# Gated attention with a channel mix: attention in 64-token halves, the fourth head pair packed into padding rows, the first group left unsplit, and all engines in one planned order

## The chip, the cores and the metric

The kernel runs on one core of a Trainium2 chip. The metric is the device time of one execution in microseconds (us), the median of several runs. The engines are TensorE (PE, matmuls), VectorE (DVE), ScalarE (ACT) and GpSimd (POOL), and each works through its own instructions in order; SyncE (SP) issues most DMAs, also in order.

## The reference

Eight heads of 48 features, four batches of 768 tokens. Per head a 48x48 state decays by `alpha` along its rows and takes up `k v^T`; the output is `q` times the state. The eight heads' outputs, side by side, are the 384 features of a channel mix.

```python
for t in range(S):                                     # attention, per batch and head
    state = alpha[t][:, None] * state + outer(k[t], v[t])
    y[t] = q[t] @ state
xk = mu_k * x + (1 - mu_k) * x_prev                    # x: y of all heads, x_prev: one token before
xr = mu_r * x + (1 - mu_r) * x_prev
k = maximum(xk @ w_k, 0)                               # 384 -> 1024
v = (k * k) @ w_v                                      # 1024 -> 384
out = sigmoid(xr @ w_r) * v
```

## The kernel before

**Groups and chunks.** The 768 tokens of a batch are six chunks of 128 tokens. Chunks form groups (`CUTS`): 2, 2, 2 in the first batch, then 3, 3 in each of the others, nine groups in all. Heads go in pairs: one head on partitions 0 to 47, the other on 64 to 111, so a tile has 112 rows (`R`), and there are four pairs (`NP`).

**Preparation of a group** (`prep_p`, `prep_gh`). A scan over the tokens gives the running product of alpha (L231), a reverse scan its inverse (L254); q and k are multiplied by these (L249, L257). Tables in `PARAM` say which products run on DVE and which on POOL. After it a chunk needs matmuls and a causal mask only.

**Attention of a chunk** (`attn`). `scores` (L318): for each pair and head a matmul of 48 rows, 128 stationary and 128 moving columns, so that the two heads use the upper and the lower rows of the array. DVE multiplies all 1024 columns by the mask (L329). `trans` (L339): four transposes of k, copied by ACT (L342). `intra` (L391; L384 in the first group): eight matmuls over 128 tokens, whose outputs are 48 or 64 columns of the array for one head and for the other. `update` (L349): eight matmuls of 48 columns, added to the state by DVE (L357). `inter` (L407): four matmuls of 112 rows with a block-diagonal state. ACT copies the result to `xt` (L417) and the fourth pair to `x3` (L416), from where two DMAs put it into the 16 free rows behind each head (L420); the first group has a form of its own without these DMAs. All attention matmuls are f32.

**Channel mix of a group** (`mix`, `moe`). ACT scales (L474), DVE adds the previous token (L479), and each x is split into a rounded part (ACT, L482) and a remainder (L484). Weights are split likewise (`split`): merge (L186), rounding (L192, L194), remainder (L195, on POOL or DVE). Each product is then three matmuls on the fast f32r form: `up` (L501), `gate` (L526), `down` (L541). Between `up` and `down`, ACT and DVE square and split again (L509 to L515). The result is gated (L546) and stored (L547).

**Order.** PE's and SP's instructions are written out by hand. At the start 22 small matmuls on zeros are issued (L98). Attention of group g+1 is woven into the channel mix of group g by weights (`merge`); in the first group, weight splits and preparations are put in at fixed positions (`PARAM['pos']`), and 19 pieces of the second group's attention and then 14 of the first group's channel mix are issued ahead of the weaving. The other engines' order is that of the calls.

Of the kernel before, what the change touches and what calls it, by code (L numbers as in the profile page):

```python
# [25 lines left out]
C = 128  # L26
CUTS = [[2, 2, 2], [3, 3], [3, 3], [3, 3]]
GROUPS = [(b, sum(cut[:i]), n) for b, cut in enumerate(CUTS) for i, n in enumerate(cut)]
NG = len(GROUPS)
GMAX = 3 * C  # L30
# [3 lines left out]
NT = 3  # L34
NF = FF // 128
# [5 lines left out]
LEAD = 12.0  # L41
PARAM = {'pos': {'wk0': 29, 'wk1': 65, 'wk2': 22, 'wk3': 29, 'wr0': 106, 'wr1': 94, 'wv0': 70, 'wv1': 75, 'wv2': 72, 'wv3': 81, 'prep10': 12, 'prep11': 61, 'prep12': 65, 'prep13': 1, 'prep20': 104, 'prep21': 92, 'prep22': 102, 'prep23': 138, 'load2': 93, 'pp1': 88, 'pp2': 118}, 'dma': ['k', 'wk0', 'al', 'wk1', 'q', 'wk2', 'wk3', 'v'], 'eng': {'wr1': 'DP', 'wk0': 'AP', 'wk2': 'AP', 'wv0': 'DP', 'wv1': 'DP', 'wv2': 'AD', 'wv3': 'DP', 'wv4': 'DD', 'wv5': 'DD', 'wv6': 'DD', 'wv7': 'DD', 'wk1': 'AD', 'wk3': 'AP', 'wk4': 'DP', 'wk5': 'DP', 'wk6': 'DP', 'wk7': 'DP', 'wr0': 'DP', 'wr2': 'AD', 'wr3': 'AD', 'wr4': 'AD', 'wr5': 'AD', 'wr6': 'AD', 'wr7': 'AD'}, 'a1': 19, 'hold': 14, 'lead0': 8.0, 'sp': 3.0, 'prep': 0.2, 'xl': 'DDD', 'k2': 'AAD', 'h': ['DDDD', 'PDPD', 'PPPP'], 'm': 'AAA', 'warm': 22, 'g': ['PDDD', 'DPDP', 'DDDP'], 'sc': 'PP', 'mm': 2, 'direct': 1, 'pad': [1.0, 1.5], 'xr': 'DDD'}
NX = HB - D


def merge(main, side, lead):
    total = max(sum(w for w, _ in main) - lead, 1.0)
    load = sum(w for w, _ in side)
    done = spent = 0.0
    side = list(side)  # L50
    for w, f in main:
        f()
        done += w
        while side and spent / load <= done / total:
            ws, fs = side.pop(0)
            fs()
            spent += ws
    for _, fs in side:
        fs()
# [3 lines left out]
def gated_attention_channel_mix(  # L63
# [3 lines left out]
    q_p: bass.AP,  # L67
    k_p: bass.AP,
# [11 lines left out]
    nc = tc.nc  # L80
    PE, ACT, DVE, POOL = nc.tensor, nc.scalar, nc.vector, nc.gpsimd

    cp = ctx.enter_context(tc.tile_pool(name="cp", bufs=1))
    p1 = ctx.enter_context(tc.tile_pool(name="p1", bufs=1))
    p2 = ctx.enter_context(tc.tile_pool(name="p2", bufs=2))
    p3 = ctx.enter_context(tc.tile_pool(name="p3", bufs=3))
    ps = ctx.enter_context(tc.tile_pool(name="ps", bufs=1, space=PSUM))
    pm = ctx.enter_context(tc.tile_pool(name="pm", bufs=3, space=PSUM))
    dp = ctx.enter_context(tc.tile_pool(name="dp", bufs=1, space=DRAM))

    sbd = [cp.tile([R, NP, R], F32, name=f"sbd{i}") for i in range(2)]
    for t in sbd:
        POOL.memset(t, 0.0)

    hot = pm.tile([R, R], F32, tag="pm", name="hot")
    with tc.manual_schedule(engines={mybir.EngineType.PE}):
        for i in range(PARAM["warm"]):
            PE.matmul(hot, sbd[1][:, 0], sbd[1][:, 0], start=True, stop=True)  # L98

    tiny = cp.tile([128, 1], F32, name="tiny")  # L100
    POOL.memset(tiny, FLOOR)
    mone = cp.tile([128, 1], F32, name="mone")
    POOL.memset(mone, -1.0)
    ones = cp.tile([128, 1], F32, name="ones")
    POOL.memset(ones, 1.0)
    ACT.activation(ones, ones, AF.Sigmoid)
    POOL.memset(ones, 1.0)
    racc = cp.tile([128, 2 * NG], F32, name="racc")
    pbeg = cp.tile([128, NG * NP], F32, name="pbeg")
    pend = cp.tile([128, NG * NP], F32, name="pend")  # L110
    pscl = cp.tile([128, NG * NP], F32, name="pscl")
    mu = cp.tile([128, 2, NT], F32, name="mu")

    loaded = {}

    def span(g):
        b, c0, n = GROUPS[g]
        return b, c0, n, n * C

    def load(g):  # L120
        b, c0, nck, n = span(g)
        al = p2.tile([R, NP, n + 1], F32, tag="al", name=f"al{g}")
        pp = p1.tile([R, NP, n], F32, tag="pp", name=f"pp{g}")
        k = p2.tile([R, NP, n], F32, tag="k", name=f"k{g}")
        q = p2.tile([R, NP, n], F32, tag="q", name=f"q{g}")
        v = p2.tile([C, nck, NP, R], F32, tag="v", name=f"v{g}")
        loaded[g] = (al, pp, k, q, v)
        at = NP * (b * S + c0 * C)
        c1 = (b * S) // C + c0

        def get(t, src, p, m):
            nc.sync.dma_start(
                t[:, p : p + m, :n],
                src[:, at + p * n : at + (p + m) * n].rearrange("r (p t) -> r p t", p=m),
            )

        parts = {
            "al": lambda p=0, m=NP: get(al, al_p, p, m),
            "k": lambda p=0, m=NP: get(k, k_p, p, m),
            "q": lambda p=0, m=NP: get(q, q_p, p, m),  # L140
            "v": lambda: nc.sync.dma_start(v, v_p[:, c1 : c1 + nck]),
        }
        if g == 0:
            for p in range(0, NP, 2):
                for x in ("al", "k", "q"):
                    parts[x](p, 2)
            parts["v"]()
        elif g > 1:
            for x in parts:
                parts[x]()  # L150
        return parts

    with tc.manual_schedule(engines={mybir.EngineType.SP}):
        load(0)

    mask = cp.tile([C, C], F32, name="mask")
    POOL.memset(mask, 1.0)
    POOL.affine_select(
        out=mask, in_=mask, pattern=[[1, C]], compare_op=ALU.is_ge, fill=0.0,
        base=0, channel_multiplier=-1,  # L160
    )
    ident = cp.tile([128, 128], F32, name="ident")
    make_identity(nc, ident)
    wkh = cp.tile([128, NT, FF], F32R, name="wkh")
    wkl = cp.tile([128, NT, FF], F32R, name="wkl")
    wvh = cp.tile([128, NF, DM], F32R, name="wvh")
    wvl = cp.tile([128, NF, DM], F32R, name="wvl")
    wrh = cp.tile([128, NT, DM], F32R, name="wrh")
    wrl = cp.tile([128, NT, DM], F32R, name="wrl")

    tops = [cp.tile([128, 2 * DM], U32, name=f"tops{i}") for i in range(2)]
    for t in tops:
        POOL.memset(t, 0)
    turn = [0]

    def split(hi, lo, raw, he, le):
        w = raw.bitcast(U32)[:, :, 1::2]
        n = w.shape[2]
# [638 lines left out]
```

## Time and profile before

| | |
|---|---|
| runs | 403.24, 403.93, 401.58 us |
| median | 403.24 us |
| profiled execution, first to last instruction (span) | 396.4 us; its whole time is not given apart |
| PE busy | 356.6 us (90%) |
| DVE busy | 287.6 us (73%) |
| ACT busy | 190.0 us (48%) |
| POOL busy | 72.4 us (18%) |
| mean granted clock of PE | 0.947 |

A busy share is the time in which at least one instruction of the engine was under way. Matmuls are pipelined, so their durations overlap and the spacing of their starts says what one costs. An f32 matmul is recorded twice. "[idle before <-X]" says how long the engine stood still ahead of an instruction and what released it.

### The profile page before, as it was taken

To read this page: it belongs to the slowest core of one execution; us is meant where nothing else is said; L and a number is where in the kernel's file an instruction comes from. 1 tells how busy PE (TensorE), PEld (TensorE's weight loads), DVE (VectorE), ACT (ScalarE), POOL (GpSimd) and SP (SyncE) were. 2 spreads that over 40 slices of the span, in tenths; PEclk is the share of its full clock that TensorE was granted. 3 is DMA by queue.
4 is the path that set the end of the run, shared out by engine and by line. 5 is a ranking of instruction groups with operands and counts; after the bars stand their busy time and mean duration, and the time that the engine had idled before them with its cause. 6 is when DMAs were issued, how large, how long until landed. Compare 5 with 4: busy or idle time off the path is not lost.

```text
span 396.4 us, 7183 instructions
## 1 busy us (share of the span) xinstructions
PE 356.6 (90%) x2834; PEld 337.8 (85%) x2834; DVE 287.6 (73%) x451; ACT 190.0 (48%) x421; POOL 72.4 (18%) x85
## 2 busy tenths in 40 slices
PE   7674987898929979999999999999999999999993
PEld 7563976787919969999989999899999999999993
DVE  5699999996995399965998399929894755374510
ACT  3256874645613474444555446436644524463500
POOL 4364465361120030400040004000210000000000
PEclk9685998789988999999999999999999999999997
DMA  8997078537030611333112510251000100001001
GB/s 211 247 339 299 1 215 224 147 103 219 20 90 2 195 32 40 80 115 102 61 34 82 182 40 21 71 154 41 21 2 17 40 21 2 15 24 38 2 21 46
DMA packets 15816, 35.82 MB, mean 90 GB/s; under 512 B 1568, under 2 KB 9440, under 8 KB 15776
## 3 DMA queue, kind: packets, MB, share of 16 engines
q1 hardware_dynamic: 14608, 34.21, 28.8%
q10 hardware_dynamic: 1168, 1.09, 1.1%
q8 instruction: 24, 0.39, 0.4%
q14 instruction: 16, 0.13, 0.1%
HBM read 29.49 MB, written 4.72 MB: 86 GB/s over the span
## 4 chain that ended last, share of the span: by engine, by line
PE 46%; DVE 35%; DMA 9%; issue 4%; ACT 3%; SPq 1%; ACTq 0%; DVEq 0%
PE pv L541 14%; PE pk L501 14%; DVE al L254 6%; PE pg L526 5%; DVE pp L231 5%; DVE x L479 4%; DMA xt<-x 4%; DVE kl L515 4%; PE py L407 4%; PE py L391 4%; DMA al<-al_p 3%; PE sp L318 3%; DVE am L329 3%; DVE q L249 2%; DVE xkl L484 2%
## 5 line engine op out<-in xcount | busy, mean ns | idle before, releaser
L541 PE MATMUL pv<-wvl,kh 128*128 128x384 f32 x192 | 65.9, 343 | 2.9 <-DVE wvl L195 2.9
L541 PE MATMUL pv<-wvh,kl 128*128 128x384 f32 x192 | 65.6, 342 | 1.9 <-DVE kl L515 1.9
L541 PE MATMUL pv<-wvh,kh 128*128 128x384 f32 x192 | 65.9, 343 | 1.1 <-ACT r L509 1.1
L509 ACT ACTIVATE r<-pk 128x384 f32<-128x384 f32 (+1 forms) x72 | 32.6, 457 | 62.3 <-PE pk L501 45.4
L515 DVE TENSOR_TENSOR kl<-k,kh 128x384 fp32r<-128x384 f32 (+1 forms) x72 | 45.4, 630 | 7.6 <-ACT kh L514 2.8
L318 PE MATMUL sp<-q,k 48*128 48x128 f32 x384 | 33.2, 312 | 18.7 <-DVE am L329 14.0
L501 PE MATMUL pk<-xkh,wkh 128*128 128x384 f32 (+1 forms) x216 | 46.8, 325 | 1.9 <-ACT xkh L482 1.4
L318 PEld LDWEIGHTS sp<-q,k 48*128 48x128 f32 x384 | 26.8, 207 | 25.4 <-DVE am L329 15.9
L501 PE MATMUL pk<-xkh,wkl 128*128 128x384 f32 (+1 forms) x216 | 47.9, 331 | 0.0
L501 PE MATMUL pk<-xkl,wkh 128*128 128x384 f32 (+1 forms) x216 | 47.5, 329 | 0.0
L257 POOL TENSOR_TENSOR k<-k,al 112x768 f32<-112x768 f32 (+1 forms) x18 | 31.7, 1762 | 74.3 <-DVE al L254 47.3
L254 DVE TENSOR_TENSOR_SCAN al<-al 112x383 f32<-112x383 f32 (+1 forms) x36 | 41.1, 1176 | 1.0 <-ACT junk L238 0.7
L513 DVE TENSOR_TENSOR k<-r 128x384 f32<-128x384 f32 (+1 forms) x56 | 30.0, 536 | 16.1 <-ACT r L509 14.0
L479 DVE SCALAR_TENSOR_TENSOR x<-xt,nu,x 128x384 f32<-128x384 f32 (+1 forms) x54 | 31.2, 605 | 11.2 <-ACT x L474 11.1
L541 PEld LDWEIGHTS pv<-wvl,kh 128*128 128x128 f32 x192 | 36.6, 191 | 3.2 <-DVE wvl L195 3.2
L541 PEld LDWEIGHTS pv<-wvh,kl 128*128 128x128 f32 x192 | 36.5, 190 | 2.5 <-DVE kl L515 2.5
L501 PEld LDWEIGHTS pk<-xkh,wkh 128*128 128x128 f32 x216 | 36.4, 192 | 2.4 <-ACT xkh L482 1.6
L541 PEld LDWEIGHTS pv<-wvh,kh 128*128 128x128 f32 x192 | 36.6, 190 | 1.6 <-ACT r L509 1.4
L474 ACT ACTIVATE x<-xt,mu 128x384 f32<-128x384 f32 (+1 forms) x54 | 29.3, 577 | 17.5 <-DMA xt<-x 10.2
L501 PEld LDWEIGHTS pk<-xkh,wkl 128*128 128x128 f32 x216 | 36.1, 194 | 1.0
L501 PEld LDWEIGHTS pk<-xkl,wkh 128*128 128x128 f32 x216 | 35.8, 192 | 0.7 <-issue 0.4
L249 DVE TENSOR_TENSOR q<-q,pp 112x768 f32<-112x768 f32 (+1 forms) x20 | 15.9, 808 | 27.5 <-DMA q<-q_p 27.5
(93 smaller groups left out, 574.5 us busy)
## 6 DMA issues: line engine op xcount, KB each, us to landing
out<-sig SPq DMA_DIRECT2D x24, 192.0 KB, 1.8
k<-k_p SPq DMA_DIRECT2D x6, 672.0 KB, 4.4
al<-al_p SPq DMA_DIRECT2D x6, 672.0 KB, 5.1
q<-q_p SPq DMA_DIRECT2D x6, 672.0 KB, 6.4
v<-v_p SPq DMA_DIRECT2D x6, 672.0 KB, 5.0
wkraw<-wk_p SPq DMA_DIRECT2D x4, 768.0 KB, 15.9
vraw<-wv_p SPq DMA_DIRECT2D x4, 768.0 KB, 7.4
v<-v_p SPq DMA_DIRECT2D x3, 448.0 KB, 7.9
```

Source lines behind the costliest of these rows:

```text
L231: DVE.tensor_tensor_scan(pp[:, p], al[:, p, :n], tiny[:R].to_broadcast([R, n]), initial=START, op0=ALU.mult, op1=ALU.max,)
L249: (DVE if PARAM["g"][min(g, 2)][p] == "D" else POOL).tensor_tensor(q[:, hp], q[:, hp], pp[:, hp], op=ALU.mult)
L254: DVE.tensor_tensor_scan(back, back, back, initial=al[:, i, n : n + 1], op0=ALU.mult, op1=ALU.bypass)
L257: (DVE if PARAM["h"][min(g, 2)][p] == "D" else POOL).tensor_tensor(k[:, hp], k[:, hp], al[:, hp, 1:], op=ALU.mult)
L318: PE.matmul(sp[c][:, j, p, :], h[r0 : r0 + D, p, c * C : (c + 1) * C], q[r0 : r0 + D, p, c * C : (c + 1) * C], start=True, stop=True,)
L474: ACT.activation(x, xt[:, t, 1 : 1 + n], AF.Copy, scale=mu[:, i, t : t + 1])
L479: DVE.scalar_tensor_tensor(x, xt[:, t, 0:n], nu[:, i, t : t + 1], x, op0=ALU.mult, op1=ALU.add)
L501: PE.matmul(pk, w[:, t, cols], x[:, t], start=part == 0 and t == 0, stop=part == 2 and t == NT - 1,)
L509: ACT.activation(r, pk, AF.Relu)
L513: DVE.tensor_tensor(k2, r, r, op=ALU.mult)
L515: DVE.tensor_tensor(kl[:, f], k2, kh[:, f].bitcast(F32), op=ALU.subtract)
L541: PE.matmul(pv, x[:, f, cols], w[:, f], start=f == 0 and i == 0, stop=f == NF - 1 and i == 2,)
```

## The change

- **Attention in halves.** Scores and intra are computed for the two diagonal 64x64 token blocks of a chunk only; the state is carried from half to half. Every step but the transposes becomes 16 matmuls on 64-row, 64-column tiles, in the order of the four tile positions. The mask covers 512 columns. `inter` uses a state of 48 rows per head, so two of the four tile positions.
- **Packing.** The fourth pair's 96 features lie in the 16 padding rows behind each head of the other three pairs, in alpha, k and q too: preparation works on three tiles of 128 partitions. Two DMA steps per group (`move`, two DMAs each) bring k and q of the fourth pair to 112 rows of their own; its output goes back with two DMAs per chunk on SP's queue (`move_y3`).
- **First group unsplit.** Group 0 uses f32 matmuls, one in place of three, with merged weights and unsplit activations; weights are split for the later groups.
- **Engines.** All products of the preparation and all remainders are on DVE. POOL keeps memsets, mask, identity and the carried column. The matmuls on zeros go.
- **Order.** `graph` lists every step with an assumed duration and its needs. PE's order is fixed by `SPOTS`: the n-th attention step ("visit") stands ahead of the channel-mix step with that number (the channel mix has 18 steps in group 0, 38 in groups 1 and 2, 45 in the others). `Plan.run` then simulates all engines, each taking the ready step with the longest way to the end, shifted by `SOONER`, and steps are issued in the order of their planned begin.

```diff
-CUTS = [[2, 2, 2], [3, 3], [3, 3], [3, 3]]
+PREP = [2, 2, 2, 3, 3, 3, 3, 3, 3]
+MIX = [2, 2, 2, 3, 3, 3, 3, 3, 3]
+FULL = (0,)
+SPOTS = [
+    0, 0, 0, 0, 0, 0, 0, 0, 3, 3, 5, 7, 9, 9, 19, 30, 32, 35, 38, 42, 46, 59, 66, 71, 75, 82,
+    86, 100, 108, 112, 115, 125, 135, 144, 152, 154, 159, 162, 169, 179, 192, 194, 201, 205,
+    231, 238, 250, 263, 264, 279, 287, 292, 302, 304, 307,
+]
...
+    def attention(c):
+        return {
+            0: [[("sc", 0), ("tr", 0)], [("sc", 1)], [("ia", 0), ("up", 0)], [("tr", 1)], [("ie", 0)]],
+            1: [[("ia", 1), ("up", 1)], [("ie", 1)]],
+            2: [[("sc", 2), ("tr", 2)], [("sc", 3)], [("ia", 2), ("up", 2), ("tr", 3)], [("ie", 2)]],
+            3: [[("ia", 3), ("up", 3)], [("sc", 4), ("tr", 4)], [("ie", 3)], [("sc", 5)]],
+        }.get(c, [[("ia", c), ("up", c), ("sc", c + 2), ("tr", c + 1)], [("ie", c)]])
...
+    def move(self, g, what):
+        n = self.size(g)
+        lo, hi = (0, n) if what == K_AT else (n, 2 * n + 1)
+        for j in range(2):
+            self.SP.dma_start(
+                self.kq3[g % 2][j * HB : j * HB + D, lo:hi],
+                self.kq[g][j * HB + D : (j + 1) * HB, :, lo:hi],
+            )
...
+    def scores(self, c):
+        sp = self.spt[c] = self.ps.tile([C, 2, 512], F32, tag="sp", name=f"sp{c}")
+        for p in range(NP):
+            for j, s in ((0, 0), (1, 1), (0, 1), (1, 0)):
+                self.PE.matmul(
+                    sp[s * HB : (s + 1) * HB, j, p * HB : (p + 1) * HB],
+                    self.kq_of(c, p, j, K_AT, s), self.kq_of(c, p, j, Q_AT, s),
+                    start=True, stop=True, skip_group_check=True,
+                )
...
+    def inter(self, c):
+        halves = (1,) if c % NCB == 0 else (0, 1)
+        for p in range(NP):
+            for i in range(len(halves)):
+                for j in range(2):
+                    s = halves[(i + j) % len(halves)]
+                    rows = slice(j * HB, j * HB + D)
+                    self.PE.matmul(
+                        self.yu[c][rows, s, p * HB : (p + 1) * HB],
+                        self.st[c, s][rows, p, :], self.kq_of(c, p, j, Q_AT, s),
+                        start=False, stop=True, skip_group_check=True,
+                    )
...
+    def factors(self, m, w, x):
+        return [(w[0], x[0])] if m in FULL else [(w[0], x[0]), (w[1], x[0]), (w[0], x[1])]
...
+    with tc.manual_schedule():
+        k = Kernel(ctx, tc, al_p, kq_p, v_p, mu_p, wk_p, wv_p, wr_p, out)
+        plan, order, _, _ = graph(SPOTS)
+        begin, _ = plan.run(order, SOONER)
+        for i in sorted(range(len(begin)), key=lambda i: (begin[i], i)):
+            if plan.jobs[i][2] is not None:
+                name, args = plan.jobs[i][2]
+                getattr(k, name)(*args)
```

## Rows read from the trace of the kernel before

**Rows 1.** The windows view: four stages (first channel-mix matmul at 41.75, last one to start before 390); per engine busy us and instructions, then PE's granted clock, DMA share and GB/s.

```profile
0.00:41.75 41.75, 28.06 (x253) 25.19 (x253) 33.99 (x49) 19.96 (x38) 20.02 (x38) 0.75 0.87 260
41.75:147.00 105.25, 86.96 (x708) 80.86 (x706) 89.36 (x143) 56.51 (x146) 33.48 (x28) 0.92 0.42 117
147.00:390.00 243.00, 241.55 (x1877) 231.80 (x1877) 163.71 (x260) 113.49 (x240) 18.93 (x19) 1.00 0.16 51
390.00:396.40 6.40, 0.00 (x0) 0.00 (x0) 0.56 (x1) 0.00 (x0) 0.00 (x0) 0.66 0.12 38
```

**Rows 2.** The chain of waits that ends last, in order of time, of the start: start, us, what.

```profile
5.33 12.90 DMA al<-al_p
18.32 2.44 DVE pp L231 x4
```

**Rows 3.** The windows view, 10 us each, columns as in rows 1.

```profile
20.00:30.00 10.00, 6.97 (x83) 6.20 (x78) 9.89 (x14) 5.06 (x10) 6.19 (x8) 0.83 1.03 344
30.00:40.00 10.00, 4.89 (x38) 4.12 (x40) 9.91 (x13) 6.99 (x14) 5.15 (x4) 0.51 0.73 285
```

**Rows 4.** The waits view of PE: who waited for whom, us in total, times, longest.

```profile
PE sp L318 <- DVE am L329: 14.0, 4, 7.8
```

**Rows 5.** The chain again, late: runs of one chunk's steps, and the last group's channel mix, into which nothing is woven.

```profile
292.81 0.56 PE pu L349 x16
...
332.69 1.09 PE sp L318 x16
...
340.95 1.02 PE py L391 x15
341.97 1.06 PE py L407 x8
...
359.54 12.57 PE pk L501 x72
372.75 4.43 PE pg L526 x24
377.18 12.81 PE pv L541 x72
```

**Rows 6.** The timeline of one chunk's attention late in the run (PEld is PE's weight load); the last row is from a window that begins at 325.98 and is 0.04 us long.

```profile
318.63 0.97 PEld L318 LDWEIGHTS sp<-q,k 48*128 48x128 f32 x16 [0.25 <-issue]
...
320.70 0.52 PEld L339 LDWEIGHTS pt<-ident,k 112*128 112x128 f32 x4
...
321.17 0.48 PEld L501 LDWEIGHTS pk<-xkh,wkh 128*128 128x128 f32 x3
...
325.98 0.53 PE L349 MATMUL pu<-v,ht 128*48 128x48 f32 x16
...
325.98 0.21 PE L349 MATMUL pu<-v,ht 128*48 128x48 f32 x2
```

**Rows 7.** The timeline of PE in the first group's `up`.

```profile
42.19 0.50 PE L501 MATMUL pk<-xkh,wkl 128*128 128x256 f32 x3
42.53 0.50 PE L501 MATMUL pk<-xkl,wkh 128*128 128x256 f32 x3
```

**Rows 8.** Groups by line, POOL and ACT: shapes xcount | busy us, mean ns | idle before.

```profile
L257 POOL TENSOR_TENSOR k<-k,al 112x768 f32<-112x768 f32 (+1 forms) x18 | 31.7, 1762 | 74.3 <-DVE al L254 47.3 <-issue 16.8 <-PE sp L318 9.4
L195 POOL TENSOR_TENSOR wvl<-vraw,wvh 128x768 fp32r<-128x768 f32 x3 | 6.7, 2247 | 4.6 <-DVE wvh L194 4.6
L195 POOL TENSOR_TENSOR wkl<-wkraw,wkh 128x768 fp32r<-128x768 f32 x3 | 5.5, 1840 | 4.2 <-ACT wkh L192 4.2
L417 ACT COPY xt<-py 112x384 f32<-112x384 f32 x22 | 10.7, 487 | 0.0
```

**Rows 9.** DVE: single operations on the timeline (start, us), then groups by line and shape (columns as in rows 8).

```profile
4.03 1.27 DVE L231 TENSOR_TENSOR_SCAN pp<-al,tiny 112x256 f32<-112x256 f32 x2 [4.03 <-DMA al<-al_p]
9.98 0.75 DVE L254 TENSOR_TENSOR_SCAN al<-al 112x255 f32<-112x255 f32 x1
10.65 0.40 DVE L249 TENSOR_TENSOR q<-q,pp 112x256 f32<-112x256 f32 x1
33.07 2.19 DVE L479 SCALAR_TENSOR_TENSOR x<-xt,nu,x 128x256 f32<-128x256 f32 x1
38.36 0.48 DVE L479 SCALAR_TENSOR_TENSOR x<-xt,nu,x 128x256 f32<-128x256 f32 x1
44.67 0.42 DVE L515 TENSOR_TENSOR kl<-k,kh 128x256 fp32r<-128x256 f32 x1
103.32 1.00 DVE L254 TENSOR_TENSOR_SCAN al<-al 112x383 f32<-112x383 f32 x1
...
L254 DVE TENSOR_TENSOR_SCAN al<-al 112x383 f32<-112x383 f32 x24 | 30.6, 1313 | 0.7 <-ACT junk L238 0.7
L329 DVE TENSOR_TENSOR am<-sp,mask 128x1024 f32<-128x1024 f32 x24 | 29.2, 1217 | 5.8 <-PE sp L318 5.7
L231 DVE TENSOR_TENSOR_SCAN pp<-al,tiny 112x384 f32<-112x384 f32 x24 | 22.1, 943 | 0.0
L357 DVE TENSOR_TENSOR sbd<-sbd,pu 48x192 f32<-48x192 f32 x32 | 11.2, 349 | 3.1 <-PE pu L349 2.8
L186 DVE SCALAR_TENSOR_TENSOR wkraw<-wkraw,tops 128x768 uint32<-128x768 uint32 x4 | 3.8, 950 | 2.2 <-ACT tops L181 2.2
```

**Rows 10.** The line that moves the fourth pair's output (L420), all 16 of its DMAs: from issue to landing, us.

```profile
DMA to landing us min/median/max: 2.5/5.5/7.0
```

More of the change, by code (lines that the diff above doesn't have):

```diff
@@ L26 @@
 C = 128
-CUTS = [[2, 2, 2], [3, 3], [3, 3], [3, 3]]
-GROUPS = [(b, sum(cut[:i]), n) for b, cut in enumerate(CUTS) for i, n in enumerate(cut)]
-NG = len(GROUPS)
-GMAX = 3 * C
+NCB = S // C
+NCH = B * NCB
 NP = H // 2
@@ L34 @@
 NT = 3
+NX = HB - D
 NF = FF // 128
@@ L43 @@
[L43 to L59, printed above, removed]
+GMAX = 3 * C
+PREP = [2, 2, 2, 3, 3, 3, 3, 3, 3]
+MIX = [2, 2, 2, 3, 3, 3, 3, 3, 3]
+RAW_AT = {
+    ("k", 0): "raw0", ("k", 1): "raw1", ("k", 2): "raw2", ("k", 3): "raw0", ("r", 0): "raw1",
+    ("r", 1): "raw2", ("v", 0): "raw0", ("v", 1): "raw2", ("v", 2): "raw2", ("v", 3): "raw2",
+}
@@ L91, in gated_attention_channel_mix @@
[L91 to L103, printed above, removed]
@@ L153, in gated_attention_channel_mix @@
[L153 to L166, printed above, removed]
@@ L424, in both @@
-        def both(c, go):
-            before[c] = state.get(b)
-            intra(c)
-            if go:
-                update(c)
-        def add(w, f, c):
-            if g > 2:
-                pieces.append((w * NP, lambda: [f(c, p) for p in range(NP)]))
-                return
-            for p in range(NP):
-                pieces.append((w, lambda p=p: f(c, p)))
-        def visit(c, go):
-            if c + 1 < nck:
-                for p in range(NP):
-                    scores(c + 1, p)
-            both(c, go)
-            for p in range(NP):
-                inter(c, p)
@@ L580, in rows @@
-    def rows(g):
-        b, c0, _, _ = span(g)
-        at = b * S + c0 * C
-        return lambda t: out[at + t * 128 : at + (t + 1) * 128, :]
-    with tc.manual_schedule(engines={mybir.EngineType.SP}):
-        first = load(1)
-        for x in PARAM["dma"]:
-            if x[0] == "w":
-                load_wk(int(x[2]))
-            else:
-                first[x]()
-    nc.scalar.dma_start(mu, mu_p)
-    nu = cp.tile([128, 2, NT], F32, name="nu")
-    POOL.tensor_scalar(nu, mu, -1.0, 1.0, op0=ALU.mult, op1=ALU.add)
@@ new lines, in fallback @@
+            POOL.tensor_copy(last, xt[:, :, GMAX:])
+            m = ("f", sc)
+            k.xt[m] = xt
+            for i in range(2):
+                for t in range(NT):
+                    k.x_mul(m, i, t)
+                    k.x_add(m, i, t)
+                    k.x_hi(m, i, t)
+                    k.x_lo(m, i, t)
+            for f in range(NF):
+                for part in range(3):
+                    k.up(m, f, part)
+                k.relu(m, f)
+                k.square(m, f, "A")
+                k.k_hi(m, f)
+                k.k_lo(m, f)
```

1507 lines of the change are left out of this document (944 added, 563 removed), and 82 rows, old and new, of the table SOONER.

## The prediction

> **What bounds the kernel now.** I read the windows of four stages first [rows 1]. From 147 to 390 us TensorE (PE) is busy for 241.6 of 243.0 us at the full granted clock: in this stage the time is PE's own work, and only shorter PE work shortens it. From 0 to 41.75 us there is no channel-mix matmul at all, and from 41.75 to 147 PE is busy for only 87 of 105 us, at a mean clock of 0.92. The chain of the start [rows 2] names DMA and then VectorE (DVE); DVE is busy for 9.9 of 10 us between 20 and 40 us [rows 3], and the largest of PE's waits is ended by DVE's mask [rows 4]. So there are two problems: before 147 us a late and interrupted start set by DVE and the loads, behind it a full PE. Then I read what PE's work costs: the channel mix from the end of the chain, where nothing is interleaved [rows 5], and attention from one chunk on the timeline [rows 6].
>
> **Two price lists for PE.** Channel mix: 72 `up` matmuls take 12.57 us, 24 of 27 `gate` matmuls 4.43 (4.98 for all), 72 `down` 12.81 [rows 5], so 30.4 us for a group of three chunks. A 384-column matmul is 12.57/72 = 0.175 us, which is 384 columns at 2.4 GHz (0.160) plus 0.015. A split 256-column matmul takes 0.113 us (one step of three starts 0.34 after the last [rows 7]), so a two-chunk group is 72 x 0.113 + 18 x 0.184 + 48 x 0.178 = 20.0 us.
>
> Attention: an f32 matmul leaves two records (16 records for 8 matmuls in `scores`), each of two passes over its columns. In the update 16 records start between 325.98 and 326.30 (0.53 less the record's 0.21 [rows 6]). Two records start together, as a window around 325.98 shows, so there are eight slots, 0.32/7 = 0.046 us apart: 48 columns x 2 passes / 2.4 GHz = 0.040, plus 0.006. The two matmuls of a slot write different column halves of the array: they run side by side. By the same sum a slot of 64 columns is 0.053 + 0.006 = 0.059. Coming from the channel mix costs about 0.25 us more (PE's weight loads stand idle for 0.25 "issue" ahead of `scores` [rows 6]).
>
> **The change, part by part.**
> *Attention tiles.* Now a chunk takes 1.09 (scores) + 0.47 (transposes, 320.70 to 321.17) + 1.02 (intra) + 0.56 (update) + 1.06 (inter) us [rows 5, 6]. Over a batch of six chunks, where the first needs no inter and the last neither update nor transposes: 6.54 + 2.35 + 6.12 + 2.80 + 5.30 = 23.1, or 3.86 a chunk. After: scores, intra, update and inter have 16 matmuls, 32 records, each. No row shows four tiles side by side. The ends are four in one slot (8 slots of 0.059) and no better than the update's full price per matmul, 0.56/8 = 0.070. I take four: rows and columns of the array both already show independent halves (scores split its rows, the update its columns [rows 6]). Scores and intra are 8 x 0.059 = 0.47 each, the update 8 x 0.046 = 0.37; inter uses only the two diagonal tiles, so 16 x 0.059 = 0.94, no gain against today; transposes 0.47; two entries (intra, update and scores stand together, inter alone) 0.50. Six chunks, with all six transposed, 5.5 updates and 5.5 inters: 2.82 + 2.82 + 2.04 + 5.17 + 2.82 + 3.00 = 18.7, or 3.11 a chunk. That is 0.75 us less per chunk, and behind 147 us, where 15 of the masks lie, 11.3 us.
>
> *First group unsplit.* Its 24 + 6 + 16 matmuls run as f32, two records of two passes: 24 x 2 x (0.213 + 0.015) + 22 x 2 x (0.320 + 0.015) = 25.7 us against 20.0, so PE pays 5.7 us. It buys that the first `up` no longer waits for split weights and activations, of which the remainder of a weight quarter alone costs 1.84 on POOL [rows 8].
>
> *Packing and engines.* Three prepared tiles instead of four take a quarter off each scan and product. All POOL work of size (k products 31.7 us, weight remainders of two kinds 12.2 [rows 8]) goes to DVE; against that the mask is half as large (1.2 us for 1024 columns, so about 0.63), and DVE's two-input operations lose a neighbour: the reverse scan means 1.31 us but took 1.00 at 103.32, and an x addition took 2.19 us at 33.07 against 0.48 [rows 9]. POOL's work is off PE's path now, so I cost its removal only through DVE. The two moves per group and one per chunk that packing adds are DMAs on SP's queue; today's moves land in 2.5 to 7.0 us, median 5.5 [rows 10]. In the full-PE stage they hide under the `down` matmuls of the group before (by the list of places the last inter of a group stands at least 10 `down` steps of 1.07 us ahead of the group that needs it; the copy's 0.49, the move's 5.5 and some 0.6 each for scaling, addition and rounding, 0.48 at 256 columns enlarged to 384, make 7.8 us [rows 8 to 10], and what exceeds the 10.7 would stop PE one for one). At the start they don't hide. SP is one queue in order: behind a blocked move wait loads, stores and weights, and with them DVE's preparations.
>
> *Start.* Planned order on PE: seven visits of chunks 0 and 1 and the scores of chunk 2 stand ahead of the first `up`. DVE starts at 4.03 [rows 9], as now. Group 0: 3 x (0.63 + 0.75 + 2 x 0.40) + 0.9 of small ones = 7.4, to 11.4 us. Until the first `up` DVE then owes group 1's preparation 7.4, two masks 1.3, four states 1.4, six x additions 2.8 and four weight merges 3.8 (0.95 each [rows 9]): 16.7, to 28.1; with scores and transposes of chunk 2 behind it, 29 us instead of 41.75. The loads needed by then (some 6.4 MB) fit: at the 260 GB/s of the stage up to 41.75 [rows 1] 7.5 MB come in 29 us. The dropped warm-up matmuls cost nothing that I can place: the clock is at its lower level (1.2 of 2.4 GHz) for parts of 20 to 40 us with them, too [rows 3].
>
> *29 us to the point that now stands at 147.* PE's need today: 20.0 + 20.0 + 15.7 (third group without its last token tile's `down`) + 22.0 of attention (nine chunks at 3.86, less 12.7 for the three and the scores of the fourth that ran before) = 77.7 of 105.25 us; 27.6 are lost to waits and the low clock. After: 25.7 + 20.0 + 15.7 + 21.8 (nine chunks at 3.11, less 6.2 that ran before 29) = 83.2. DVE owes until then: four preparations 31.8 (three at 7.4, one at 3 x (0.94 + 1.00 + 2 x 0.48) + 0.9), weights 22.8 (merges and remainders of nine and a half pieces at 0.95 each, five roundings at no more than that), nine masks 5.7, 18 states 6.3, 18 x additions at 0.48 and 12 remainders at 0.42 13.7, 16 k remainders 6.7 [rows 9], six gatings 3.4 (0.56 in the last stage [rows 1]): 90, of which 24 lie before 29 us. That leaves 66 of 93 us, against 89.4 busy of 105.25 today, so I let a bit over a third of the loss remain: 10 us (bounds 0 and 27.6).
>
> **Sum.** 29 + (83.2 + 10) + (243.0 - 11.3) + 6.4 (last `down` to the end [rows 1]) = 360.3 us of span. The profiled execution's own time isn't given apart from its span of 396.4; the median of the runs, 403.24, is 6.8 above that, and I add the same: **367 us**.
>
> **Rivals.**
> 1. *Records bind, not columns.* If PE can't start records faster than the update does, 0.046/2 = 0.023 us each, 32 of them are 0.74 for scores, intra and update instead of 0.47, 0.47 and 0.37: 0.91 more per chunk, on the 22 chunks behind the start 20 us: 387. For it: no row has a faster series. Against it: two records start together, so the spacing is the columns' doing. The Trainium skill ("TensorE: Matmul & The Clock Gate", section "Wait — 56ns, not 53.3ns?") gives a floor of about 25 ns from start to start however small N is; the update's mean of 23 ns lies there, its pairs far under it.
> 2. *Slower: only two tiles at a time.* Place: the four small-tile steps of every chunk. Then a matmul's price lies on the line through today's two, 0.070 at 48 columns and 1.09/8 = 0.136 at 128 (entry included): 0.083 at 64. A chunk has 61.3 of them on average: 5.1 + 0.47 = 5.56 us, 2.45 more than forecast, x 22 = 54: 421 us. It is slower from 1.65 us per chunk on, or 0.070 per matmul, which is just the update's price. For it: every row has two. Against: halves by rows and halves by columns both work.
> 3. *A late start.* If each of the two moves on the start's path lands like the loads around it (12.9 us for al at 5.33 [rows 2]) instead of about 4, the first `up` is at 45: 383 us. For it: one queue, filled with weights. Against: the weights past the first two wait for the moves' issue.
> That the change doesn't do what it says I exclude for work that is visibly gone; the planner's times may be wrong, which is the 10 us of stalls.
>
> **Chances.** Forecast 0.57 (its own range 352 to 380: first `up` 24 to 34, stalls 0 to 18), rival 1 0.15, rival 3 0.16, rival 2 0.12. To leave out 2 in 10 at most, the range reaches from 349, over rivals 1 and 3, to 394. About 0.5% is what a measurement here can tell from no change; so faster is 0.85, from the forecast and from rivals 1 and 3 apart; same 0.03, where rivals 1 and 3 come together (367 + 20 + 16 = 403); slower 0.12, from rival 2.
>
> **What would show it.** Right: the first `up` near 29 us; a visit's 96 records of scores, intra and update in about 1.5 us; inter near its 1.06; a PE over 97% busy for the last 230 us and groups 2 us apart less than today's 41; DVE rows of reverse scan near 1.0. Wrong: 32 records in over 0.7 us (rivals 1 and 2, apart by whether four, or two, start together); a first `up` past 38 behind a move's landing (rival 3); waits for DVE in PE's list well over 10 us between 29 and 120, or SP's queue holding a move.

## The result, and the profile after

The changed kernel takes 362.19 us (median of 4 runs, 361.3 to 365.02); the kernel before took 402.41 beside it (400.49 to 403.93). The ratio is 0.9016, interval 0.8953 to 0.908: 10% faster. The forecast was 367 us, with a range from 349 to 394. The profiled execution of the changed kernel has a span of 363.2 us and took 365.02.

The page of the changed kernel, its span and its engines:

```profile
span 363.2 us, 10432 instructions
...
PE 332.8 (92%) x4436; PEld 308.2 (85%) x4436; DVE 240.8 (66%) x508; ACT 184.8 (51%) x393; POOL 6.9 (2%) x35
```

Its windows, with the stages of [rows 1]: to the first channel-mix matmul; to the start of the last token tile's `down` of the third group (the point that stood at 147); the stage with a full PE; the end. Then ten microseconds of the start. Columns as in [rows 1].

```profile
0.00:36.90 36.90, 14.51 (x285) 12.14 (x285) 24.14 (x57) 14.33 (x24) 4.82 (x22) 1.00 0.77 249
36.90:128.40 91.50, 89.79 (x1403) 77.16 (x1402) 73.89 (x163) 57.92 (x141) 1.32 (x7) 1.00 0.47 147
128.40:357.00 228.60, 228.48 (x2753) 218.88 (x2751) 142.23 (x289) 112.60 (x229) 0.80 (x6) 1.00 0.19 58
357.00:363.20 6.20, 0.00 (x0) 0.00 (x0) 0.53 (x1) 0.00 (x0) 0.00 (x0) 0.73 0.13 38
...
10.00:20.00 10.00, 5.67 (x127) 5.00 (x128) 4.30 (x6) 4.40 (x5) 0.26 (x2) 1.00 0.96 328
```

Against [rows 1] the start is 4.85 us shorter (41.75 to 36.90), the middle 13.75 (105.25 to 91.50), the full stage 14.4 (243.0 to 228.6) and the end 0.2: together the 33.2 us between the spans. The middle is where the kernel changed its nature: PE is now busy for 89.8 of 91.5 us there (87.0 of 105.25 before). Only the start is still a stage in which PE waits; its last row says that DVE stands still for more than half of the time from 10 to 20 us (in the kernel before it had hardly a gap from 20 to 40 us [rows 3]). The PE clock column can't be used before 39 us: it shows 1.00, yet 32 score records take 1.13 us at 16.71 and 0.69 at 41.94 (first and third PE row below). The trace has no clock record before about 39 us.

The medians lie 40.2 us apart, the spans 33.2. The rest is which execution was profiled: span to time is 1.8 us in the changed kernel (363.2 to 365.02), so the profiled execution of before took about 398.2, below its median; that of after lies above its own.

PE's waits, columns as in [rows 4], and its timeline around the first `up`:

```profile
PE sp L922 <- DVE kq L814: 10.9, 3, 8.3
PE sp L922 <- DMA kq<-kq: 9.7, 3, 4.3
```

```profile
16.71 1.13 PE L922 MATMUL sp<-kq 48*64 48x64 f32 x32
...
35.31 0.85 PE L922 MATMUL sp<-kq 48*64 48x64 f32 x8 [4.13 <-DMA kq<-kq]
...
36.90 5.12 PE L1089 MATMUL pk<-xkh,wk 128*128 128x256 f32 x18
41.94 0.69 PE L922 MATMUL sp<-kq 48*64 48x64 f32 x32
```

The mask, the largest waker in [rows 4], has left the list. What remains is the first preparation (8.3, before which nothing can run) and the landing of moves (`kq<-kq`): 4.1 of those us stand right ahead of the first `up`.

The chain of waits of the changed kernel: the start, then one visit in the full stage.

```profile
12.29 7.81 DMA al<-al_p
20.12 0.69 DVE pp L784
...
32.04 3.18 DMA kq<-kq
35.31 0.85 PE sp L922 x8
...
183.34 0.62 PE yu L953 x30
183.97 0.38 PE yu L965 x25
...
184.42 0.48 PE sp L922 x28
184.90 0.54 PE pt L938 x4
...
188.06 1.03 PE yu L978 x32
```

Intra (L953, with the entry), update (L965) and scores (L922) together take 1.56 us, from 183.34 to 184.90; transposes 0.53, inter (L978) 1.03. DVE's groups, columns as in [rows 8]:

```profile
L1064 DVE SCALAR_TENSOR_TENSOR x<-xt,nu,x 128x384 f32<-128x384 f32 x36 | 21.3, 611 | 9.2 <-ACT x L1060 9.1
L801 DVE TENSOR_TENSOR_SCAN pp<-al,inv 128x384 f32<-128x384 f32 x18 | 17.5, 1003 | 0.0
...
L930 DVE TENSOR_TENSOR am<-sp,mask 128x512 f32<-128x512 f32 x24 | 16.5, 686 | 5.2 <-PE sp L922 4.7
```

The reverse scan means 1.00 us (1.31 in [rows 9]), the mask 0.69 (1.22).

### The profile page after: what moved, and what is told of

It is laid out like the page before. It is cut to its first block, busy times and chain, and to the rows that moved or that the text cites. A ratio compares the mean times of both kernels' runs of the same rounds, so it can differ in the third digit from the quotient of the medians.

```text
span 363.2 us, 10432 instructions
## 1 busy us (share of the span) xinstructions
PE 332.8 (92%) x4436; PEld 308.2 (85%) x4436; DVE 240.8 (66%) x508; ACT 184.8 (51%) x393; POOL 6.9 (2%) x35
## 4 chain that ended last, share of the span: by engine, by line
PE 76%; DVE 9%; DMA 8%; SPq 2%; ACT 2%; issue 1%; DVEq 0%; ACTq 0%
PE pk L1089 27%; PE pv L1156 23%; PE pg L1133 9%; PE yu L978 6%; DMA al<-al_p 4%; PE yu L953 4%; PE pt L938 3%; PE sp L922 3%; DMA xt<-x 3%; PE yu L965 2%; DVE pp L801 2%; DVE kq L814 1%; DVE x L1064 1%; DMA kq<-kq_p 1%; DMA kq<-kq 1%; DVE kq L809 1%
## 5 line engine op out<-in xcount | busy, mean ns | idle before, releaser
L1156 PE MATMUL pv<-wvh,kh 128*128 128x384 f32 x176 | 59.7, 339 | 0.0
L1156 PE MATMUL pv<-wvl,kh 128*128 128x384 f32 x176 | 59.5, 338 | 0.0
L1105 DVE TENSOR_TENSOR k<-r 128x384 f32<-128x384 f32 x48 | 26.8, 558 | 32.9 <-ACT r L1097 32.7
L1089 PE MATMUL pk<-xkh,wkl 128*128 128x384 f32 (+1 forms) x192 | 41.7, 325 | 0.0
L922 PE MATMUL sp<-kq 48*64 48x64 f32 x768 | 21.5, 237 | 21.4 <-DVE kq L814 10.9
L1122 DVE TENSOR_TENSOR kl<-k,kh 128x384 fp32r<-128x384 f32 (+1 forms) x64 | 33.3, 522 | 10.0 <-ACT k L1103 5.5
L922 PEld LDWEIGHTS sp<-kq 48*64 48x64 f32 x768 | 17.2, 142 | 23.9 <-DVE kq L814 12.3
L1118 ACT ACTIVATE kh<-r 128x384 fp32r<-128x384 f32 (+2 forms) x72 | 34.8, 487 | 1.7
L1064 DVE SCALAR_TENSOR_TENSOR x<-xt,nu,x 128x384 f32<-128x384 f32 (+1 forms) x48 | 26.6, 578 | 10.2 <-ACT x L1060 10.2
L978 PEld LDWEIGHTS yu<-kq,st 48*48 48x48 f32 x704 | 22.2, 124 | 7.1 <-DVE st L991 2.6
L784 DVE TENSOR_TENSOR_SCAN pp<-al,tiny 128x384 f32<-128x384 f32 (+1 forms) x27 | 22.4, 858 | 8.2 <-DMA al<-al_p 5.1
```

The lines of the kernel that those rows point to most:

```text
L784: self.DVE.tensor_tensor_scan(self.pp[g][:, t], self.al[g][:, t, :n], self.tiny.to_broadcast([128, n]), initial=START, op0=ALU.mult, op1=A ...
L922: self.PE.matmul(sp[s * HB : (s + 1) * HB, j, p * HB : (p + 1) * HB], self.kq_of(c, p, j, K_AT, s), self.kq_of(c, p, j, Q_AT, s), start=Tr ...
L978: self.PE.matmul(self.yu[c][rows, s, p * HB : (p + 1) * HB], self.st[c, s][rows, p, :], self.kq_of(c, p, j, Q_AT, s), start=False, stop=Tr ...
L1064: self.DVE.scalar_tensor_tensor(x, xt[:, t, 0 : xt.shape[2] - 1], self.nu[:, i, t : t + 1], x, op0=ALU.mult, op1=ALU.add)
L1089: self.PE.matmul(pk, w[:, t, f * 128 : (f + 1) * 128], x[:, t], start=part == 0 and t == 0, stop=part == len(pairs) - 1 and t == NT - 1,)
L1105: self.DVE.tensor_tensor(k2, r, r, op=ALU.mult)
```

## The experiments

Each edits the changed kernel unless it says otherwise; L numbers of a variant are shifted by its own lines.

### How many tiles run side by side: two and one

Scores, intra and update keep their matmuls; only the order of the tile positions changes. In the first variant only two alternate at a time, in the second one position does all four pairs before the next.

```diff
+def tile_order():
+    return [(p, a, b) for part in (((0, 0), (1, 1)), ((0, 1), (1, 0))) for p in range(NP) for a, b in part]
...
-        for p in range(NP):
-            for j, s in ((0, 0), (1, 1), (0, 1), (1, 0)):
+        for p, j, s in tile_order():
+            if True:
```

> The changed kernel, but scores, intra and update go through the tile positions in two passes: first all four pairs on the two diagonal tiles, then on the two others, so that at most two tiles can run side by side. Same matmuls, same count. Theory (four tiles run side by side, a slot costs its columns): scores and intra go from 8 to 16 slots of 0.059 us, +0.47 each, the update from 8 to 16 of 0.046, +0.37: 1.3 us per chunk, 22 chunks on a full PE, 28 us: 388 to 393 us. Rival (records bind, not columns): the order changes nothing, 361 to 365 us.

> As two_tiles, but one tile position after the other (each through all four pairs), so that nothing runs side by side in scores, intra and update. Theory: 32 slots each of 0.059, 0.059 and 0.046 us instead of 8: +1.4, +1.4 and +1.1 us, 3.9 per chunk, x 22 = 86: about 448 us. Rival (records bind): 361 to 365 us; if two tiles at most ever run side by side, this costs as much over two_tiles as scores do in the kernel before against a single tile, and two_tiles costs nothing.

Two: 373.8 us (372.93 to 374.89), ratio to before 0.9347 (0.9306 to 0.9388). One: 410.52 (408.58 to 411.48), ratio 1.0246 (1.0194 to 1.0299). The chain of the two-tile kernel, then of the one-tile kernel, one visit in the full stage:

```profile
187.47 0.73 PE yu L957 x23
...
188.37 0.39 PE yu L969 x15
...
188.94 0.59 PE sp L926 x25
189.53 0.53 PE pt L942 x4
...
192.72 1.03 PE yu L982 x32
```

```profile
211.85 1.25 PE yu L957 x28
...
213.27 0.81 PE yu L969 x24
...
214.26 1.15 PE sp L926 x29
...
218.61 1.03 PE yu L982 x32
```

The same 96 records take 1.56 us in the order of four tiles, 2.06 in two passes (187.47 to 189.53) and 3.56 in four (211.85 to 215.41). So the order of the tiles is worth 48 us of the time, and with it the sign: in the last order the kernel is 2.5% slower than before. But both variants cost less than I expected: 11.6 us instead of 28 for two, 48 instead of 86 for one. The timeline of the one-tile kernel says why. Its rows are a stretch of the visit above, then the last four scores records of that visit; the row behind them is from scores of the changed kernel.

```profile
213.98 0.22 PE L926 MATMUL sp<-kq 48*64 48x64 f32 x1
213.99 0.22 PE L969 MATMUL yu<-v,ht 64*64 64x48 f32 x1
214.04 0.22 PE L926 MATMUL sp<-kq 48*64 48x64 f32 x1
214.04 0.22 PE L969 MATMUL yu<-v,ht 64*64 64x48 f32 x1
...
215.02 0.39 PE L926 MATMUL sp<-kq 48*64 48x64 f32 x4
```

```profile
184.24 0.66 PE L922 MATMUL sp<-kq 48*64 48x64 f32 x30
```

The first scores records (L926) start between the last ones of the update (L969): two positions are at work at once, and each series keeps some 0.05 to 0.06 us from start to start. The last four records have nothing beside them and start 0.058 us apart (0.39 less the 0.22 of one record, for three steps). That is the forecast's slot of 0.059. On four tiles 30 records start within 0.44 us, which is 0.061 for four. Eight scores records on one tile then need 0.46 us, but the twelve turns of a visit, four positions in each of three steps, take 3.56/12 = 0.30 each: a position begins before the last one is done. So neither variant holds PE to two tiles or to one. My prices for them failed on what the edit does, not on what a tile costs.

### First group split as the others

The first group gets the three-matmul form back; the list of visits is mapped to its 54 steps.

```diff
-FULL = (0,)
+FULL = ()
```

> The changed kernel with the first group split like the others: 18 steps of it become 38, and the places of attention behind them move along. PE saves 5.7 us of work; weights and activations must be split before the first up is complete, and shared buffers (merged weights lie where the first remainders go) make the remainders wait for all of a weight. Theory (leaving it unsplit is worth more than it costs): the first up's group stretches over DVE's splits, 4 to 12 us slower, 366 to 374. Rival (the unsplit group is no gain): 356 to 362 us.

378.47 us (375.92 to 380.19), ratio 0.94 (0.9333 to 0.9467): 16 slower than the changed kernel, more than expected, though PE has less to do. Its windows from the first `up` to the point that is 128.4 in the changed kernel, with the full stage behind, its largest wait of PE behind the start, and two of the three times that make it up:

```profile
35.61:143.50 107.89, 90.17 (x1447) 84.24 (x1446) 79.14 (x178) 63.09 (x156) 0.98 (x7) 0.87 0.40 125
143.50:372.10 228.60, 228.60 (x2754) 219.31 (x2753) 142.28 (x287) 112.57 (x229) 1.20 (x6) 1.00 0.19 58
```

```profile
PE pk L1088 <- ACT xkh L1068: 17.1, 3, 8.2
```

```profile
80.03 0.98 PE L1088 MATMUL pk<-xkh,wkh 128*128 128x256 f32 x2 [4.84 <-ACT xkh L1068]
85.10 0.58 PE L1088 MATMUL pk<-xkh,wkh 128*128 128x256 f32 x1 [4.10 <-ACT xkh L1068]
```

The first `up` isn't later (35.61), but after two matmuls it waits 8.2 us for ScalarE's rounding, and the stage is 16.4 longer at a clock of 0.87; the full stage is the same to 0.1. The unsplit group pays PE and buys the middle. Not all of the 16 us is the split's own price: the other 8.9 us of the wait (80.03 and 85.10) stand ahead of the second group's `up`, which is split in the changed kernel too. There the rounding waits for DVE, which does the fourth group's preparation first, as in *Alpha first* below. How much a plan of its own would save I didn't try.

### All q and k products on DVE, in the kernel before

```diff
-'h': ['DDDD', 'PDPD', 'PPPP'],
+'h': ['DDDD', 'DDDD', 'DDDD'],
...
-'g': ['PDDD', 'DPDP', 'DDDP'],
+'g': ['DDDD', 'DDDD', 'DDDD'],
```

> The kernel before with all products of the preparation (q and k) on DVE, none on POOL; weight remainders stay. Theory (POOL's work slows DVE's two-input operations as much as it relieves it): DVE gains about 17 us of work and loses about 20 of stretching (reverse scans 24 x 0.3, k remainders 48 x 0.12, others); time within 4 us of the kernel before. Rival (POOL truly relieves a bound DVE in the first 147 us): 8 to 15 us slower.

397.32 us (394.18 to 398.65, 7 runs), ratio 0.9921 (0.9882 to 0.996): 0.8% faster than before. Its DVE, columns as in [rows 8]:

```profile
L254 DVE TENSOR_TENSOR_SCAN al<-al 112x383 f32<-112x383 f32 x24 | 23.6, 1004 | 0.7 <-ACT junk L238 0.7
```

The same line means 1.313 in [rows 9]. POOL's products, 31.7 us for k alone [rows 8], went to DVE, and DVE's own busy time fell (281.1 against 287.6). POOL had relieved DVE of nothing. The mean of 1.313 hides two kinds of scan. In the kernel before, all 36 scans of this line (shortest, median and longest in ns):

```profile
L254 DVE TENSOR_TENSOR_SCAN al<-al x36: 717/1005/2305, 5.6 to 284.5; 112x383 f32<-112x383 f32 x24, 112x255 f32<-112x255 f32 x12
```

The median is 1.005 us and the longest 2.305; with the products on DVE the longest is 1.017.

The Trainium skill ("SBUF — State Buffer", section "SBUF: two separate sides") says that a VectorE operation with two inputs in SBUF and a GpSimd operation that reads SBUF need the same pair of ports, and whichever starts first holds it for its whole instruction. The rows agree: most scans beside POOL's work keep their 1.0 us, and some take more than twice that.

### The planner's shifts

```diff
-SOONER = {
-    "al_one 1": -59, "al_one 2": 2.5, "al_one 3": -14, "al_one 5": -12, "al_one 6": -21.5,
...
+SOONER = {}
```

> The changed kernel with an empty table of shifts (SOONER): PE's order stays, the other engines' order is by the longest way to the end alone. Theory (behind the start PE is full, and the other engines have room: DVE 66% busy): up to 5 us slower, 362 to 367, with PE's waits still under 20 us. Rival (the shifts carry the tight order): over 372 us, with new waits of PE for DVE or DMA all along the run.

363.01 us (361.55 to 364.56), ratio 0.9056 (0.9009 to 0.9104): the same as with them.

### The start: seven variants

The first `up` came 7.9 us later than forecast. In the changed kernel SP issues the moves of group 0 from 8.43 and group 1's alpha at 12.29; it lands 7.81 later, and DVE can't prepare group 1 until then (chain above). The variants change the clock, this order or the queue.

*Warm*: some 60 unused matmuls fill PE's waits ahead of the first `up`.

> The changed kernel with about 60 f32 matmuls on the identity (128 columns, result unused) put between the first attention visits, so that PE hardly stands still before the first up. Theory (up to 37 us attention runs at the lower clock level: 32 scores 1.13 us against 0.69 later, and DVE twice waits 1.4 us for a state): the visits take half, the first up comes 2 to 3 us earlier and its first 18 matmuls save 0.9: 358 to 360 us. Rival (the start is bound by loads alone): within 1 us of 362, or slower where the added matmuls stand in the way.

362.87 us (361.58 to 364.33). The first 18 `up` matmuls take 4.06 us instead of 5.12, and nothing else moves (first `up` at 36.63). The low clock costs 1 us in this stretch, and the time doesn't show it.

*Early alpha*: alpha, k and q of group 1 are loaded at once, ahead of the moves of group 0 (alpha into a buffer of its own); and the same with the warm matmuls.

```diff
-        behind = issued[:]
+        behind = issued[:] if g > 1 else []
...
-            self.al[g] = self.p1.tile([128, NT, self.size(g) + 1], F32, tag="al", name=f"al{g}")
+            self.al[g] = self.p1.tile([128, NT, self.size(g) + 1], F32, tag="kh" if g == 1 else "al", name=f"al{g}")
```

> The changed kernel; alpha of group 1 gets a buffer of its own (the one that the first group's squares use later), and the loads of alpha, k and q of group 1 no longer wait for group 0's scans and moves; they are also ranked earlier. Theory (the first up comes at 36.9 instead of 29 because DVE sits idle until alpha of group 1 lands at 20.1): the scan of group 1 starts near 12, the first up comes at 30 to 32, and the time falls by 4 to 7 us, to 355 to 358. Rival (behind it the next late thing stands at the same place: slow attention matmuls at the low clock, or k, q and weights that now land later): less than 2 us.

> early_al1 and warm together. Theory: what holds the start is first the late alpha, then PE's low clock; both gains add up, first up at 28 to 30 us, 352 to 355 us. Rival: one of them hides the other, no better than the better of the two.

381.87 us (380.69 to 383.8), 384.35 with the warm matmuls: 20 us slower than the changed kernel, where I had expected a gain. PE's waits in the early-alpha kernel:

```profile
PE pk L1089 <- DVE xkh L1064: 11.3, 1, 11.3
PE sp L922 <- DMA kq<-kq: 10.8, 1, 10.8
...
PE pk L1089 <- ACT xkh L1069: 7.0, 3, 4.8
```

Alpha is there (its scan starts at 15.41, not 20.12), but now the moves are behind the loads: PE stands 10.8 us for group 0's, x of the first group is late by 11.3, and the first `up` stands at 47.4. That is rival 3's late start, produced by hand; it had put the first `up` at 45 and the time at 383.

*Moves on ScalarE's queue*: the moves of group 0 and of the outputs of chunks 0 and 1 leave SP.

```diff
-            self.SP.dma_start(
+            (self.ACT if g == 0 else self.SP).dma_start(
...
-            self.SP.dma_start(
+            (self.ACT if c < 2 else self.SP).dma_start(
```

> The changed kernel with the moves of group 0 (k and q of the fourth pair) and of chunks 0 and 1's output issued by ScalarE instead of SP, so that they don't stand behind loads in SP's queue; order otherwise the same. Theory (the start is held by alpha of group 1, whose load is issued behind the moves and the weights): SP is free for that load about 3 us earlier, the scan of group 1 starts at 17 instead of 20.1, the first up comes 1 to 3 us earlier: 359 to 361 us. Rival (the moves' own landing holds the start, as in early_al1, where they waited 10.8 us): scores end at 13 instead of 15.8 and the first up comes 4 us or more earlier, 356 to 358.

363.54 us (362.74 to 364.09): no change. Its largest gap of PE behind the first preparation, and its first `up`:

```profile
18.77 1.01 PE L922 MATMUL sp<-kq 48*64 48x64 f32 x8 [7.46 <-DMA kq<-kq]
...
36.65 5.75 PE L1089 MATMUL pk<-xkh,wk 128*128 128x256 f32 x18
```

Another queue didn't take the moves past the loads: PE now waits 7.5 us for them (4.3 before). Some of that is their issue, which ends at 12.97 on ScalarE's queue and at 11.54 on SP's in the changed kernel. With the changed kernel's loads at 328 GB/s from 10 to 20 us (windows above), the rest fits bytes being moved by the same DMA engines, not SP's order; I didn't measure it apart.

*Alpha first*: group 1's alpha, k and q directly behind group 0's loads, most weights behind the moves.

> The changed kernel with alpha of group 1 in a buffer of its own and loaded right behind group 0's loads; k and q of group 1 and all weights but the first quarter stay behind group 0's moves, k and q first. That puts 0.4 MB less ahead of the moves than in the changed kernel, against 1.2 MB more in early_al1. Theory (early_al1 lost because its loads stood ahead of the moves, not because an early alpha is worth nothing): moves land by 14.5, the scan of group 1 starts near 11 and its products near 17, the first up comes at 31 to 33: 356 to 359 us. Rival (whatever comes early, something else of the same 6 MB comes late, here the weights, so the start is bound by the rate of the loads): first up within 2 us of 36.9, 360 to 364 us.

370.76 us (370.22 to 374.23), ratio 0.9269 (0.9221 to 0.9316): slower than theory and rival both had it. The scan of group 1 starts at 11.56 (20.12 before), yet the first `up` moves by only 2.3 us, to 34.58: a move's landing holds PE for 5.1 us ahead of it. Then more than that is given back: the stretch that took 91.5 takes 99.4 (34.58 to 134.0), with two waits for ScalarE's rounding (2.83 and 4.34 us, before 71.15 and 76.27) and a clock of 0.93. The rounding (ACT L1069) waits in turn for DVE's x additions (L1064), and DVE has the fourth group's preparation (L801) ahead of them. In the changed kernel, second below, the additions come first:

```profile
64.24 2.83 DVE L801 TENSOR_TENSOR_SCAN pp<-al,inv 128x384 f32<-128x384 f32 x3
...
70.68 0.81 ACT L1069 ACTIVATE xkh<-x 128x256 fp32r<-128x256 f32 x2 [6.53 <-DVE x L1064]
```

```profile
64.90 0.88 DVE L1064 SCALAR_TENSOR_TENSOR x<-xt,nu,x 128x256 f32<-128x256 f32 x2 [0.41 <-ACT x L1060]
...
69.29 2.83 DVE L801 TENSOR_TENSOR_SCAN pp<-al,inv 128x384 f32<-128x384 f32 x3
```

*No moves*: the moves of groups 0 and 1 are left out, in the changed kernel and in alpha first.

```diff
     def move(self, g, what):
+        if g < 2:
+            return
```

> The four DMA pairs that bring q and k of the fourth pair of groups 0 and 1 to their own rows are left out, so these two groups' fourth pair contributes nothing; every other instruction and the order stay. Theory (loads and moves share one stream, and the moves cost twice: SP stands 3.1 us in them ahead of group 1's alpha, and PE waits for their landing): alpha of group 1 is issued near 9.2 instead of 12.29 and its scan begins near 17 to 18 instead of 20.1, PE's 4.1 and 4.3 us waits for the moved rows vanish, the first up stands at 30 to 32 instead of 36.9, and the time falls to 357 to 359. Rival (the loaded bytes set the start, the moves lie beside them): alpha lands at 19 to 20 whenever it is issued, the first up moves by less than 2.5 us, and the time stays within 2 of 362.

> al1_first without the moves of groups 0 and 1, otherwise the same. Theory: with alpha early (scan near 11.6) and no move to wait for, the start is what DVE owes, and the first up comes at 28 to 30, as the prediction's sum had it (34.6 less the 5.1 us wait and something of DVE's); behind it the rounding of the activations and the weights that were put off cost their 7 us all the same, so the time is 364 to 367. Rival (bytes): the first up stays at 33 or later.

362.26 us (361.68 to 362.88) and 370.58 (368.74 to 371.13). Without moves alone the first `up` stands at 33.88, 3.0 earlier, but the span is only 2.0 shorter (361.2) and the time is not lower at all: between theory and rival, and the time is the rival's (the runs of the changed kernel itself have spans of 359.6 to 363.2). SP issues group 1's alpha at 10.28 here, at 12.29 in the changed kernel. Now a weight piece holds the start: its load is issued at 5.01 and lands 9.14 later, and the mask waits on DVE behind its merge. The windows of the second variant, start and middle:

```profile
10.00:20.00 10.00, 6.22 (x144) 5.27 (x144) 8.69 (x22) 3.50 (x5) 0.10 (x1) 1.00 1.05 387
20.00:30.00 10.00, 3.47 (x132) 2.94 (x132) 9.16 (x21) 6.50 (x13) 0.36 (x1) 0.94 0.65 218
...
31.13:132.20 101.07, 92.89 (x1398) 79.41 (x1399) 72.79 (x160) 56.69 (x140) 1.59 (x6) 0.93 0.42 131
```

With alpha early and no move to wait for, DVE works for 8.7 and 9.2 of 10 us and the first `up` comes at 31.13: the start that the forecast had worked out. And it gains nothing, for the middle grows from 91.5 to 101.1, with DVE in the same order as in alpha first; the time is above the expected 364 to 367, too. No variant beat the changed kernel. All keep the places of attention that were planned for it.

## Why the prediction came out right, and where its steps failed

| term | forecast | profiled execution after |
|---|---|---|
| first `up` | 29 | 36.9 |
| to the point that was 147 | 83.2 + 10 = 93.2 | 91.5 |
| full PE | 243.0 - 11.3 = 231.7 | 228.6 |
| end | 6.4 | 6.2 |
| span | 360.3 | 363.2 |
| span to time | 6.8 | 1.8 (365.0; median 362.2) |

The sum holds because errors of both signs stand in it: start +7.9, middle -1.7, full stage -3.1, offset -5.0. That they nearly cancel is luck; the total doesn't confirm its terms.

**Attention tiles: right in price and in reason.** "0.47 each" for scores and intra, 0.37 for the update and an entry of 0.25 make 1.56 for a visit; the chain shows 1.56. Inter, for which I forecast no gain, went from 1.06 to 1.03. The two-tile and one-tile runs show that side by side is what makes it. The slot under the price, two passes of 64 columns, 0.059 us on each tile, is in the rows as well: 0.058 on a tile with nothing beside it, 0.061 for four records on four tiles. Inter, on two tiles, needs 16 such slots, 0.93 us, and takes 1.03 with its entry. Four tiles at a time was a choice between two ends, since no row of before had shown it.

**Full stage.** I took 11.3 us off; 14.4 went. By its averages per chunk the forecast had 15 scores, 15 intra, 13.75 updates, 13.75 inters and 15 transposes behind this point; the windows by line count 12, 14, 12.5, 13 and 13 there. At the forecast's own prices that is 4.0 us less, moved into a middle that at 98% busy still held them, so the places of attention account for the 3.1. The 0.9 left over I can't place.

**First group unsplit.** The price was right: 18 `up` records take 4.06 us in *Warm*, some 0.22 each against 0.228. The 5.7 us that PE pays were worth it: splitting the group again costs 16 us, of which 8.2 are a wait in that group and some are the order that was kept. The forecast had put the gain into the start; split_first shows it in the middle (its first `up` isn't later).

**Stalls.** "I let a bit over a third of the loss remain: 10 us" was too many: PE misses 1.7 us of 91.5, and the first 18 `up` at the low clock cost about 1 more. This is a sum mis-sized, not a mechanism: DVE's work in the stage is 73.9 us, more than the 66 that I had summed up, and still PE hardly waits for it.

**Start: the step that failed** is "Until the first `up` DVE then owes group 1's preparation 7.4 ... 16.7, to 28.1". It lets DVE work without gaps. The amount is right, 7.4 and 16.7 us forecast and 24.1 busy up to the first `up`. But from 10 to 20 us DVE is busy for 4.3: alpha of group 1 is issued at 12.29 and lands at 20.1. It is issued late because it goes into the buffer that group 0's scans read until about 9.7, and stands behind group 0's moves (10.28 without them). The prediction says that "behind a blocked move wait loads, stores and weights, and with them DVE's preparations", but the sum of the start has no term for it. The row that bore on it stood in front of me: 12.9 us for al at 5.33 [rows 2]. no_moves_al1_first, where neither alpha nor moves come late, reaches 31.1, two from the forecast's 29; so the sum of DVE's work was right and its cover was missing. "The loads needed by then fit" by bytes; by order they didn't.

**Packing.** The moves land in 2.2 to 6.2 us with a median of 2.7 (forecast 5.5), the output moves in a median of 2.0, and PE has no wait for either behind 57 us, as forecast for the full stage (two output moves of 3.4 and 6.2 us lie on the chain at 60.8 and 87.5). DVE's scan loses POOL as a neighbour, as said: 1.00 us. The x additions mean 0.61 at 384 columns.

**The offset.** "I add the same", 6.8, was the difference between a median and one execution that is not of that median. All later pairs of span and time lie 1.7 to 2.1 apart.

**Rivals.** Rival 1 (0.023 us per record at least) is out: 28 score records in 0.48 us are 0.017, 25 of the update in 0.38 are 0.015. The Trainium skill ("TensorE: Matmul & The Clock Gate", section "Wait — 56ns, not 53.3ns?") states a floor of about 25 ns from start to start; across four tiles these rows lie under it, and the measurement decides.

Rival 2 named what the gain hangs on, how many tiles run at a time, but its price was too high: inter, which has two tiles, takes 1.03/16 = 0.064 us per matmul, and the line through a 48- and a 128-column matmul had 0.083. Two tiles at a time in the stream give 373.8, not 421, and the sign turns only in the one-tile order.

Rival 3's late start came true by half (7.9 of its 16 us), through alpha as well as the moves, and the other terms hid it in the total. Where it came true in full, in early alpha, the time was 381.87, near its 383. (Its two moves at 12.9 instead of about 4 make 17.8 us, not the 16 that it adds.) The other way a start doesn't count one for one: no_moves took 3.0 off the first `up` and nothing off the time.

Why the middle gives back what a shorter start gains can be read in part. In alpha first and its variant without moves PE waits 7.2 and 8.2 us in all for ScalarE's rounding of the second group's x, which waits for DVE, and DVE has the fourth group's preparation ahead. Open stays whether another order would keep the gain; I tried none.

## What to carry to other kernels

Small matmuls on independent tiles of the array are worth their count only if neighbours in the instruction stream lie on different tiles: the same matmuls took 1.56, 2.06 or 3.56 us by order alone. A variant that is to hold an engine to less has to be checked in the trace for doing so: the one-tile order didn't. When a start is summed up from one engine's work, look for the landing of each input that work needs, and put the loads it needs in order against the small moves that have to land among them. And a shorter start counts only as far as the next stage has its own inputs ready: 2 to 6 us gained ahead of the first channel-mix matmul never reached the end.

## What the hardware showed that I had not expected

On one 64x64 tile a 64-column f32 record starts 0.058 us after the last, and four tiles keep nearly that pace side by side (0.061 for four records). Some of this comes without any interleaving: in the one-tile order the next position starts before the last is done, so a visit takes 3.56 us, where its records one behind the other would take about 5.2 (an estimate: 64 at 0.058 and 32 of the update at the 0.046 of the forecast's slot). A reverse scan of 1.0 us on DVE took up to 2.3 beside POOL's products while its median stayed at 1.0; by the mean of 1.313 I estimate that about a quarter of the scans were hit. Small moves of 24 to 72 KB land in 2.0 to 2.7 us by the median over a run, but behind the loads of the start PE stood up to 10.8 us for one, and on ScalarE's queue 7.5.
